# Order of k's transposes and scale sums in a shared PSUM bank, and a longer conversion pipeline for the second half of w_out

## The chip, the cores and the metric

The kernel runs on one core of one Trainium2 chip (trn2). The metric is the device time of one execution in microseconds; for the kernel before, the median of three runs is 1304.76 us (1302.74 to 1306.25). A profile is taken of one execution of its own, and every time in the trace counts from the start of that execution's span.

The engines are named as the profile names them: PE is the matrix engine (PEld its weight loads), ACT the scalar engine, DVE the vector engine, POOL the general one, SP the queue that issues the DMAs. Each engine works through its own instructions in the order in which the program lists them, and semaphores hold an instruction back until what it needs is done.

## The reference

Attention with a sigmoid in place of the softmax, and behind it a two-layer network whose activation is h - tanh(h):

```python
scores = scale * np.matmul(q, k.transpose(0, 1, 3, 2)) - np.log(S)   # q, k, v: (8, 12, 448, 64)
attn = 1.0 / (1.0 + np.exp(-scores))
attn_out = np.matmul(attn, v)
x = attn_out.transpose(0, 2, 1, 3).reshape(B * S, H * D)              # (3584, 768)
h = x @ w_in                                                          # w_in: (768, 2048)
g = h - np.tanh(h)
out = g @ w_out                                                       # w_out: (2048, 768)
```

All of it is float32 in and out. The weights w_in and w_out arrive as 8-byte words (the host views float64 data as uint64), and the kernel turns them into float32 with integer operations.

## The kernel before, in words

**Numbers in two halves.** Most products run in float16 with each operand split into a high and a low half, `F*S` rounded and the rest, where S is a power of two. So each operand needs a scale, and each scale comes from a bound on its size: a sum of squares or of magnitudes. For q, k and v of a pair of heads the sums of squares are made by ACT (`norms`, lines 299 to 306), and one small matmul with a matrix of ones adds them over the partitions and hands the total to all 128 partitions (`scales`, line 313, two or three columns). A chain of tiny instructions makes the scales from it: ACT's Relu (line 315, tile `tn`), then on DVE lines 97, 318, 320, 322 and 326. `parts` (lines 329 to 338) uses them to write the two halves of K or Q out of the transposed tile.

**Batches.** There are 8 batches. The attention of batch 0 runs first, in float32, while w_in is converted (`attention32`). From then on the work is pipelined over batches: while the two layers of batch b run on PE (`moe1` or `moe1_32` for h and g, `moe2` for the output), the attention of batch b+1 is done in pieces by a generator, `stream` (lines 424 to 529). It treats 42 pairs of heads (g = 0 to 41, six for each of the batches 1 to 7). For batch 1 the weights a stay float32 (`av32`, line 393); from batch 2 on they are split too (`split_a`, `av`, lines 371 to 389).

**One pair of heads** is two blocks of `stream` (lines 502 to 527). The block with i = 1 first turns k of the pair two ahead (`turn_k`, line 448), the block with i = 0 turns q of the next pair (line 507). Then come two score tiles (`scores`, line 359), their sigmoids on ACT (`weigh`, line 368), the halves of K or Q (lines 334, 336, 337), the products with v of the block before (`do_av`), and for i = 1 the squares of the pair three ahead.

**The bank.** `turn_k` takes one PSUM tile, `kT`, of the pool tag `tr`, of which there is one buffer: one bank of 512 float32. Its columns 0 to 447 receive the four transposes of k (line 296), its columns 448 to 450 the sums (lines 312, 313). In the kernel before, `turn_k` calls `scales` first, so the small matmul is ahead of the transposes on PE, and `scales` also lists ACT's Relu, which reads columns 448 to 450 of the same bank. The framework that places the semaphores treats accesses to one bank by different engines as ordered, whatever the columns. The next tile with the tag `tr` (`qT`, or the next `kT`) has to wait until DVE has read the low half of K or Q out of the one before it (line 337).

**The conversion of w_out** (`convert`, lines 194 to 206) is a software pipeline over 16 pieces for each half of the columns. Its stages for one piece are a load (`conv_load`, DMA on SP), a step of waiting, `conv_sign` (ACT, line 145, writes the tile `stb`), `conv_bits` (DVE, lines 150, 151 and 154; it works on `stb` in place and writes `wo`), a step of waiting, and `conv_end` (line 177: a matmul of ones with `stb`, which adds the magnitudes over the partitions into the tile `wl`). For the first half there are two steps of waiting behind the load. In the first half the tile `stb` lies in buffers of other names; in the second it takes one of the eight buffers of the tag `x`, which also hold the attention outputs of the next batch.

**What sets the order.** The order on PE, ACT, DVE and POOL is the order of the program text; nothing reorders it. In the output layer of batch 0, which the function `first` (line 874) prepares and `second` (line 930) runs, each step is six matmuls (`moe2`, line 786), and a list of events, sorted by a number, says what is slipped in after which step: a block of `stream` after the steps 2, 5, 8, 12, 16, 20, 24, 31 and 38 (`BLOCKS0`), a step of the conversion after each of the steps 1 to 19 (`CONV` = 1.0, 19 of them), splits of w_out's first half after k + 0.5, splits of w_in from 16 on, each 0.78 later (`SPLIT`), the scale of w_out's second half at 19 (`w_out_scale(1)`, which reads `wl`), and from 19.5 on its splits. An event runs after the first step whose count is not below its number. Before that list, `first` runs four blocks of `stream` back to back, with the rest of batch 0's activation between them.

For the later batches `batch` (line 909) does the same with fewer events: blocks after the steps 8, 12, 16 and so on, and the tail of the activation after the steps 1 to 5.

The functions that the diff touches, and what calls them:

Of the kernel before, what the change touches and what calls it, by code (L numbers as in the profile page):

```python
# [34 lines left out]
class Builder:  # L35
# [2 lines left out]

    INIT = (0, 2, 3, 4, 5, 6, 7)
    SPLIT = 16, 0.78  # L40
    CONV = 1.0

    BLOCKS = (8, 12, 16, 20, 24, 28, 32, 36, 40, 44, 48, 52)
    TAIL = (1, 2, 3, 4, 5)
# [149 lines left out]
    def convert(self, part):  # L194

        ps = []
        for k, (q, staged) in enumerate(part):
            ps.append({"piece": q, "k": k, "staged": staged})
        end = [self.conv_norm, None, self.conv_end] if ps[0]["staged"] else [None, self.conv_end]
        wait = [None] * (1 if ps[0]["piece"][2] else 2)  # L200
        stages = [self.conv_load] + wait + [self.conv_sign, self.conv_bits] + end
        for t in range(len(ps) + len(stages) - 1):
            for k in range(len(stages) - 1, -1, -1):
                if stages[k] and 0 <= t - k < len(ps):
                    stages[k](ps[t - k])
            yield 1
# [217 lines left out]
    def stream(self):  # L424

        NP = self.NP
        G = (self.B - 1) * NP  # L430
        at = lambda g: (1 + g // NP, g % NP)
        splits = lambda g: at(g)[0] >= self.AV32
        qk, v, ss, sc, K, Q, vv = {}, {}, {}, {}, {}, {}, {}

        def load(g):
            if g < G:
                qk[g] = self.load_qk(*at(g))
                if splits(g):
                    v[g] = self.load_v(*at(g), self.nat, "vn", 2)

        def norms(g):
            if g < G:
                ss[g] = self.norms(qk[g] + ([v[g]] if splits(g) else []))

        def turn(g, n, name):
            return self.transpose(qk[g][n], name) if g < G else None

        def turn_k(g):
            if g >= G:
                return None  # L450
            t = self.ps.tile([P, 512], F32, name="kT", tag="tr", bufs=1)
            sc[g] = self.scales(ss.pop(g), t)
            return self.transpose(qk[g][0], "kT", t=t)

        def parts_k(g, t):
            if g < G:
                K[g] = self.parts(t, sc[g][0][:, 0:1], "K", not splits(g) and g not in (2, 3))

        def parts_q(g, t):
            if g < G:  # L460
                Q[g] = self.parts(t, sc[g][0][:, 1:2], "Q", True)
                qk.pop(g)

        def prep_v(g):
            if g >= G:
                return
            if splits(g):
                vv[g] = self.prep_v(v.pop(g), sc[g][0])
            else:
                vv[g] = self.load_v(*at(g), self.att, "vhl", 3)  # L470

        load(0)
        load(1)
        yield 0, False
        norms(0)
        norms(1)
        yield 0, False
        for g in range(2):
            parts_k(g, turn_k(g))
            yield 450, False  # L480
            parts_q(g, turn(g, 1, "qT"))
            load(g + 2)
            yield 450, False
        norms(2)
        norms(3)
        yield 0, False
        todo = []

        def do_av():
            for g, c, A in todo:  # L490
                if c == 0:
                    self.acc = self.ps.tile([P, 512], F32, name="acc", tag="av", bufs=1)
                    if g % NP == 0:
                        self.xs = []
                (self.av if splits(g) else self.av32)(c, self.acc, vv[g], A)
                if c == 3:
                    self.xs.append(self.evac_x(g % NP, self.acc, sc[g][1][:, 1:2] if splits(g) else None))
                    for d in (sc, K, Q, vv):
                        d.pop(g)
            todo.clear()  # L500

        for g in range(G):
            for i in range(2):
                if i:
                    t = turn_k(g + 2)
                elif g:
                    t = turn(g + 1, 1, "qT")
                pss = [self.scores(c, K[g], Q[g]) for c in (2 * i, 2 * i + 1)]
                aa = [self.weigh(pss[0], sc[g][1][:CK, 0:1])]
                if i:  # L510
                    parts_k(g + 2, t)
                elif g:
                    parts_q(g + 1, t)
                aa.append(self.weigh(pss[1], sc[g][1][:CK, 0:1]))
                do_av()
                if i == 0:
                    if g == 0:
                        prep_v(0)
                    prep_v(g + 1)
                if splits(g):  # L520
                    aa = [self.split_a(a) for a in aa]
                todo.extend((g, 2 * i + n, a) for n, a in enumerate(aa))
                if g and i == 0:
                    load(g + 3)
                elif g:
                    norms(g + 3)
                yield 2750, True
        do_av()
        yield 1150, True
# [344 lines left out]
    def first(self, rest):  # L874

        n = 4
        next(self.tail)
        self.w_out_scale(0)
        ahead = [self.split_w_out(0)]
        for k in range(n):  # L880
            next(self.blocks)
            for _ in range(2):
                next(self.tail, None)
            if k == 1:
                next(ahead[0])
            if k == 2:
                self.finish_g()
                next(ahead[0])
        next(ahead[0])
        next(rest)  # L890
        next(ahead[0])
        next(rest)
        assert n + len(self.BLOCKS0) + len(self.BLOCKS1) == 4 * self.NP + len(self.BLOCKS) - self.ALONE
        split = self.split_w_in()
        at, each = self.SPLIT
        events = [(at + k * each, lambda: next(split, None)) for k in range(self.NC * self.NB + 1)]
        events += [(k + 0.5, lambda: next(ahead[0], None)) for k in range(self.NF // 2 - 3)]
        steps = self.NF + 3
        events += [(k * self.CONV, lambda: next(rest, None)) for k in range(1, steps + 1)]
        at = math.ceil(steps * self.CONV)  # L900

        def scale():
            self.w_out_scale(1)
            ahead[0] = self.split_w_out(1)

        events += [(at, scale)] + [(at + 0.5 * k, lambda: next(ahead[0], None)) for k in range(1, self.NF // 2 + 1)]
        self.second(0, self.BLOCKS0, 2 * self.NP - n, events)
# [72 lines left out]
```

## Time and profile before

| what | value |
|---|---|
| median of three runs | 1304.76 us |
| the profiled execution: its own time | 1303.86 us |
| its span, first to last instruction | 1301.7 us |
| mean granted clock of PE | 0.990 |
| matmuls po, line 786, 2304 of them | 391.5 us |
| matmuls ph, line 668, 2016 of them | 382.6 us |
| matmuls sc, line 359, 1008 of them | 117.0 us |
| transposes kT, line 296, 168 of them | 26.1 us |
| sums in kT, line 313, 84 matmuls for 42 calls | 12.6 us |
| column sums wl, line 177, 32 of them | 10.5 us |

The page gives the busy time of each engine and, for groups of instructions, how long the engine sat idle before them and what ended that. The view of waits sums these idle times by waiter and by what it waited for; it can be asked for a stretch of time. The timeline lists instructions in order with the idle time before them in brackets. Matmuls overlap, so the shown duration of one is longer than the distance from its start to that of the next: six po matmuls take about 1 us of PE, not six times 326 ns.

In time the span falls into: batch 0's attention (to 67 us), the first layer of batch 0 in float32 (67 to 154), four blocks back to back (154 to 180), the output layer of batch 0 with the conversion (180 to 284), and then for each of the batches 1 to 7 a first layer of about 56 us and an output layer that holds the blocks of the batch after it.

### The profile page before, as it was taken

To read this page: it belongs to the slowest core of one execution; us is meant where nothing else is said; L and a number is where in the kernel's file an instruction comes from. 1 tells how busy PE (TensorE), PEld (TensorE's weight loads), DVE (VectorE), ACT (ScalarE), POOL (GpSimd) and SP (SyncE) were. 2 spreads that over 40 slices of the span, in tenths; PEclk is the share of its full clock that TensorE was granted. 3 is DMA by queue.
4 is the path that set the end of the run, shared out by engine and by line. 5 is a ranking of instruction groups with operands and counts; after the bars stand their busy time and mean duration, and the time that the engine had idled before them with its cause. 6 is when DMAs were issued, how large, how long until landed. Compare 5 with 4: busy or idle time off the path is not lost.

```text
span 1301.7 us, 20443 instructions
## 1 busy us (share of the span) xinstructions
PE 1246.9 (96%) x8011; PEld 684.5 (53%) x8011; DVE 953.9 (73%) x1488; ACT 934.4 (72%) x1311; POOL 38.3 (3%) x38
## 2 busy tenths in 40 slices
PE   9898889899899999999999999999999999999998
PEld 3244434455555555555555655555555555555555
DVE  4989888869865798566975769666985769735940
ACT  5957666858888687876877868876887768762830
POOL 0100000000000000000000000000000000000000
PEclk9999989999999999999999999999999999999999
DMA  9952145110022200221012200221002110000001
GB/s 252 291 139 77 43 131 154 41 33 2 22 63 63 54 1 16 62 56 40 1 48 62 57 7 1 62 63 47 1 22 69 50 33 1 27 13 19 1 13 31
DMA packets 114367, 70.52 MB, mean 54 GB/s; under 512 B 91872, under 2 KB 104416, under 8 KB 114272
## 3 DMA queue, kind: packets, MB, share of 16 engines
q1 hardware_dynamic: 114272, 69.23, 20.0%
q8 instruction: 63, 1.03, 0.3%
q14 instruction: 32, 0.26, 0.1%
HBM read 58.20 MB, written 11.01 MB: 53 GB/s over the span
## 4 chain that ended last, share of the span: by engine, by line
PE 77%; ACT 9%; DVE 8%; issue 3%; DMA 2%; SPq 1%; DVEq 0%; ACTq 0%
PE ph L668 29%; PE po L786 21%; PE sc L359 7%; PE acc L383 6%; PE por L824 5%; PE ph L698 3%; ACT a L368 2%; PE kT L296 2%; DMA raw<-moe_w_in 1%; PE acc L393 1%; ACT ahl L374 1%; PE qT L296 1%; DVE m L738 1%; DVE m L749 1%; DVE m L752 1%
## 5 line engine op out<-in xcount | busy, mean ns | idle before, releaser
L786 PE MATMUL po<-wo,g 128*128 128x384 f16 x2304 | 391.5, 326 | 1.0 <-ACT o L815 1.0
L668 PE MATMUL ph<-xhl,wi 128*128 128x448 f16 x2016 | 382.6, 352 | 0.0
L786 PEld LDWEIGHTS <-g 128*128 128x128 f16 x2304 | 219.4, 98 | 172.8 <-issue 32.3
L668 PEld LDWEIGHTS <-wi 128*128 128x128 f16 x2016 | 196.7, 98 | 185.0 <-issue 1.8
L368 ACT ACTIVATE a<-sc,nls,rn 112x896 f32<-112x896 f32 x168 | 180.2, 1095 | 91.6 <-PE sc L359 78.4
L375 DVE SCALAR_TENSOR_TENSOR ahl<-a,ahl 112x896 f16<-112x896 f32 x144 | 155.7, 1122 | 67.2 <-ACT ahl L374 67.2
L734 ACT ACTIVATE u<-ph,ih 128x896 f32<-128x896 f32 x64 | 64.5, 1008 | 106.1 <-PE ph L668 94.7
L374 ACT ACTIVATE ahl<-a 112x896 f16<-112x896 f32 x144 | 128.0, 939 | 0.0
L359 PE MATMUL sc<-Q,K 64*112 64x448 f16 x1008 | 117.0, 366 | 2.3 <-ACT a L368 2.3
L738 DVE SCALAR_TENSOR_TENSOR m<-ph,ihk,u 128x896 f32<-128x896 f32 x64 | 73.5, 1148 | 59.1 <-ACT th L736 58.8
L383 PE MATMUL acc<-ahl,vhl 112*64 112x448 f16 x864 | 95.5, 357 | 0.0
L652 ACT ACTIVATE g<-m,Sg 128x896 f16<-128x896 f32 x64 | 66.6, 1041 | 32.3 <-DVE m L752 27.1
L752 DVE COPY_PREDICATED m<-u,th 128x896 f32<-128x896 uint32 x64 | 77.2, 1206 | 6.9 <-ACT u L734 0.5
L653 DVE SCALAR_TENSOR_TENSOR g<-m,Sg,g 128x896 f16<-128x896 f32 x64 | 73.4, 1147 | 9.6 <-ACT g L652 9.5
L337 DVE SCALAR_TENSOR_TENSOR Q<-qT,sn,Q 128x448 f16<-128x448 f32 x42 | 28.7, 682 | 70.3 <-ACT Q L334 70.3
L359 PEld LDWEIGHTS <-K 64*112 64x112 f16 x1008 | 60.2, 129 | 36.7 <-issue 6.0
L698 PE MATMUL ph<-x,wi 128*128 128x448 f32 x192 | 76.8, 550 | 0.0
L749 DVE SCALAR_TENSOR_TENSOR m<-q,m 128x896 f32<-128x896 f32 x64 | 69.9, 1093 | 8.1 <-ACT q L748 0.7
L739 DVE SCALAR_TENSOR_TENSOR th<-ph,ih,th 128x896 f32<-128x896 f32 x64 | 73.2, 1144 | 0.0
L745 DVE SCALAR_TENSOR_TENSOR m<-q,m 128x896 f32<-128x896 f32 x64 | 69.5, 1087 | 0.0
L751 ACT ACTIVATE u<-u,b 128x896 f32<-128x896 f32 x64 | 66.7, 1043 | 3.5 <-DVE m L738 1.5
L383 PEld LDWEIGHTS <-vhl 112*64 112x64 f16 x864 | 42.8, 109 | 46.2 <-issue 24.3
(134 smaller groups left out, 1324.9 us busy)
## 6 DMA issues: line engine op xcount, KB each, us to landing
raw<-moe_w_in SPq DMA_DIRECT2D x24, 512.0 KB, 6.3
rawo<-moe_w_out SPq DMA_DIRECT2D x32, 384.0 KB, 3.8
kn<-k SPq DMA_DIRECT2D x96, 112.0 KB, 2.8
qn<-q SPq DMA_DIRECT2D x96, 112.0 KB, 2.8
vn<-v SPq DMA_DIRECT2D x48, 224.0 KB, 2.6
out<-o SPq DMA_DIRECT2D x7, 336.0 KB, 3.2
out<-o SPq DMA_DIRECT2D x7, 288.0 KB, 3.0
out<-o SPq DMA_DIRECT2D x7, 240.0 KB, 2.6
```

The costliest lines, as they stand in the source:

```text
L359: nc.tensor.matmul(ps[:CK, h, :S], K[r, w, cs], Q[r, x, :], start=(n == 0), stop=(n == len(prods) - 1))
L368: nc.scalar.activation(a, ps[:CK, :, :S], AF.Sigmoid, bias=self.nls[:CK], scale=scale)
L374: nc.scalar.activation(A[:, 0], a, AF.Copy, scale=A_SCALE)
L375: nc.vector.scalar_tensor_tensor(A[:, 1], a, A_SCALE, A[:, 0], op0=ALU.mult, op1=ALU.subtract)
L383: nc.tensor.matmul(acc[h * D : (h + 1) * D, : self.S], v[:, w, h, c, :], A[:, x, h], start=(c == 0 and n == 0), stop=(c == 3 and n == 2),)
L653: nc.vector.scalar_tensor_tensor(g[:, 1], m, Sg, g[:, 0], op0=ALU.mult, op1=ALU.subtract)
L668: nc.tensor.matmul(ph[:, e, :S], self.wi[:, c * self.NB + k, part, e * P : (e + 1) * P], xhl[c][:, x, :], start=(i == 0), stop=(i == 3 * s ...
L698: nc.tensor.matmul(ph[:, e, :S], self.where("in", c)[:, f * P : (f + 1) * P], xs[c], start=(c == 0), stop=(c == self.NC - 1),)
L738: V.scalar_tensor_tensor(m, ps, ihk, u, op0=ALU.mult, op1=ALU.mult)
L749: V.scalar_tensor_tensor(m, q2, C2, m, op0=ALU.add, op1=ALU.mult)
L752: V.copy_predicated(m, u.bitcast(U32), th)
L786: nc.tensor.matmul(po[i][:, :H], gs[f // 2][:, x, f % 2, tk * P : (tk + 1) * P], self.wo[:, i * self.NF + f, w], start=(f == 0 and n == 0) ...
```

## The change

In `turn_k` the four transposes are listed first, and `scales`, with the small matmul and all that hangs on it, behind them. Both still go to the same tile. In `convert` the pipeline for the second half of w_out gets one more step of waiting between `conv_bits` and `conv_end`; for the first half and for w_in the list of stages comes out as it was. The conversion then has 20 steps behind the first two instead of 19, and `CONV` = 0.95 puts the twentieth at 19.0, where the nineteenth was; the steps 1 to 19 still fall after the same matmul steps.

```diff
-    CONV = 1.0
+    CONV = 0.95
...
-        end = [self.conv_norm, None, self.conv_end] if ps[0]["staged"] else [None, self.conv_end]
-        wait = [None] * (1 if ps[0]["piece"][2] else 2)
+        end = [self.conv_norm if ps[0]["staged"] else None, None, self.conv_end]
+        wait = [None, None]
+        if not ps[0]["staged"]:
+            (wait if ps[0]["piece"][2] else end).remove(None)
         stages = [self.conv_load] + wait + [self.conv_sign, self.conv_bits] + end
...
             t = self.ps.tile([P, 512], F32, name="kT", tag="tr", bufs=1)
+            turned = self.transpose(qk[g][0], "kT", t=t)
             sc[g] = self.scales(ss.pop(g), t)
-            return self.transpose(qk[g][0], "kT", t=t)
+            return turned
...
-        steps = self.NF + 3
+        steps = self.NF + 4
```

`NF` is 16. The code looks at the first piece of a conversion: its `piece[2]` is 0 for w_in and for the first half of w_out, and 1 for the second half of w_out; `staged` is true for w_in alone.

## The prediction

> **What bounds the kernel now.** I read the page first, then the waits of PE, over the whole span and by stretches, then the timeline around single turns of k.
>
> ```profile
> span 1301.7 us, 20443 instructions
> PE 1246.9 (96%) x8011; PEld 684.5 (53%) x8011; DVE 953.9 (73%) x1488; ACT 934.4 (72%) x1311; POOL 38.3 (3%) x38
> ```
>
> PE is busy for 1246.9 of 1301.7 us, so 54.8 us is all that waiting can give back, apart from matmuls that run slowly. The waits of PE over the whole span:
>
> ```profile
> PE kT L296 <- ACT tn L315: 32.5, 42, 3.6
> PE wl L177 <- DVE stb L151: 4.5, 3, 2.7
> ```
>
> All 42 turns of k wait: the transposes stand behind ACT's Relu, which reads three columns of their bank. That is 32.5 us, over half of PE's idle time. The same view for 340 to 1302 us (the later batches), then for 100 to 272 us (batch 0 with the conversion):
>
> ```profile
> PE kT L296 <- ACT tn L315: 17.9, 34, 2.2
> ...
> PE kT L296 <- ACT tn L315: 14.6, 8, 3.6
> PE wl L177 <- DVE stb L151: 3.6, 2, 2.7
> ```
>
> So there are two cases: 34 turns with short waits (17.9 us) and 8 turns with long ones (14.6 us). They have to be costed apart, because the other engines are loaded differently. The busy times by stretch (length, then PE, PEld, DVE, ACT, POOL, and the granted clock):
>
> ```profile
> 100.00:154.50 54.50, 51.14 (x152) 26.56 (x150) 50.37 (x71) 37.40 (x54) 0.00 (x0) 0.97 0.24 67
> 154.50:180.50 26.00, 17.70 (x89) 7.95 (x88) 17.81 (x37) 19.22 (x26) 0.00 (x0) 0.74 0.22 62
> 180.50:201.00 20.50, 17.45 (x104) 8.99 (x103) 18.33 (x40) 13.16 (x25) 1.22 (x1) 0.92 0.59 183
> 100.00:272.00 172.00, 150.73 (x748) 78.55 (x747) 143.58 (x276) 124.82 (x213) 4.93 (x4) 0.93 0.30 87
> 340.00:1146.00 806.00, 788.10 (x5489) 448.07 (x5487) 598.13 (x889) 626.48 (x866) 25.01 (x22) 1.00 0.15 37
> ```
>
> In the later batches DVE is busy for 598.13 of 806 us and ACT for 626.48: PE alone is the bound, and what PE does not wait is gained. From 100 to 272 us DVE has 143.58 of 172, in single stretches 92% and 89%: there a wait removed from PE can come back as a wait for DVE.
>
> **The change part by part: the 34 later turns.** One of the ordinary turns, PE and the engines that answer, then PE's weight loads, and at last a column sum and the product behind it:
>
> ```profile
> 532.37 0.28 PE L313 MATMUL kT<-ss,onesf 112*128 112x3 f32 x2
> 532.69 0.26 ACT L315 ACTIVATE tn<-kT,tiny 128x3 f32<-128x3 f32 x1 [0.45 <-PE kT L313]
> 533.01 0.60 PE L296 MATMUL kT<-ident,kn 112*128 112x112 f32 x4 [0.35 <-ACT tn L315]
> 533.54 1.34 PE L359 MATMUL sc<-Q,K 64*112 64x448 f16 x12
> 534.36 2.09 ACT L368 ACTIVATE a<-sc,nls,rn 112x896 f32<-112x896 f32 x2 [1.40 <-PE sc L359]
> ...
> 532.21 0.35 PEld L313 LDWEIGHTS kT<-ss,onesf 112*128 112x128 f32 x2
> ...
> 198.73 0.33 PE L177 MATMUL wl<-stb,onesb 128*128 128x384 bf16 x1
> 198.91 1.14 PE L786 MATMUL po<-wo,g 128*128 128x384 f16 x6
> ```
>
> Before, 1.17 us pass from the sums (532.37) to the scores (533.54): 0.64 for sums and wait, 0.53 for the transposes. After, the transposes start at once, take the same 0.53, and the pair of small matmuls follows. What that pair costs between transposes and scores no row shows. From below: 0.17, the length of a column-sum step (198.73 to 198.91), since two matmuls with two loads will not beat one with one. From above: 0.45, both loads (0.35) and 0.1 until the scores' first weights are in. I take 0.35, the two loads, which is nearest because the matmuls of three columns hardly stream. So an ordinary turn goes from 1.17 to 0.88 and saves 0.29 of its 0.35 of waiting; each turn pays 0.06 for the pair having lost the cover of the wait. Over 34 turns that is 17.9 - 34 x 0.06 = 15.9 us, with the ends 17.9 + 34 x 0.12 = 22.0 and 17.9 - 34 x 0.16 = 12.5.
>
> [...]
>
> Next in line behind the moved pair: ACT's Relu waits for it, and behind Relu in ACT's queue stand the sigmoids. The sums now end 0.53 later, so Relu starts at about 532.37 + 0.53 + 0.32 + 0.03 = 533.25 and ends at 533.5. The sigmoid waits for its scores anyway; they move 0.29 earlier, from 534.36 to 534.07. So Relu is hidden with some 0.55 us to spare. DVE's scale chain and K come later by the same 0.55, but K of this pair is needed two pairs on, and the tag's buffer only by the next block's turn of q. Nothing else moves on any queue: `scales` issues no DMA.
>
> Where the wait was long, ACT was late, and something else may be late next. The worst of the later turns:
>
> ```profile
> 344.28 0.24 ACT L315 ACTIVATE tn<-kT,tiny 128x3 f32<-128x3 f32 x1
> 344.57 0.60 PE L296 MATMUL kT<-ident,kn 112*128 112x112 f32 x4 [2.16 <-ACT tn L315]
> 345.93 2.09 ACT L368 ACTIVATE a<-sc,nls,rn 112x896 f32<-112x896 f32 x2 [1.41 <-PE sc L359]
> 349.18 2.08 DVE L375 SCALAR_TENSOR_TENSOR ahl<-a,ahl 112x896 f16<-112x896 f32 x2
> 352.32 1.33 PE L383 MATMUL acc<-ahl,vhl 112*64 112x448 f16 x12
> ```
>
> PE gains about 2.1 us here, so the products at 352.32 would come at 350.2. Their second half needs what DVE finishes at 351.26, and DVE runs without a pause before that; it would be wanted at 350.85. So 0.4 to 0.5 us is given back. ACT gains 1.41 at the same time, because the scores are ready when it comes out of Relu; so its backlog shrinks and the next turns are clean. Later batches: 15.9 - 0.5 = 15.4 us.
>
> **The 8 early turns and the column sums.** Four blocks back to back (154 to 180), then the conversion:
>
> ```profile
> 161.58 1.01 PE L296 MATMUL kT<-ident,kn 112*128 112x112 f32 x4 [2.89 <-ACT tn L315]
> 162.52 2.49 PE L359 MATMUL sc<-Q,K 64*112 64x448 f16 x12
> 163.93 2.22 ACT L368 ACTIVATE a<-sc,nls,rn 112x896 f32<-112x896 f32 x2 [2.40 <-PE sc L359]
> 176.70 2.22 ACT L368 ACTIVATE a<-sc,nls,rn 112x896 f32<-112x896 f32 x2 [2.40 <-PE sc L359]
> 191.84 0.33 PE L177 MATMUL wl<-stb,onesb 128*128 128x384 bf16 x1 [2.69 <-DVE stb L151]
> 198.04 0.68 DVE L337 SCALAR_TENSOR_TENSOR K<-kT,sn,K 128x448 f16<-128x448 f32 x1 [0.71 <-ACT K L334]
> 201.20 0.55 PE L296 MATMUL qT<-ident,qn 112*128 112x112 f32 x4
> ```
>
> From 154.5 to 180.5 PE and ACT wait for each other in turn: PE 2.89 for Relu, then ACT 2.40 for scores that run at half pace (2.49 against 1.34 above, clock 0.74). With the transposes first, the scores are done before ACT gets to Relu, so ACT loses neither 2.40: gain 4.8. ACT's idle time, 26.00 - 19.22 = 6.8, is the upper end, one of the two, 2.4, the lower.
>
> From 100 to 154.5 two of the turns lie in a stretch in which DVE has 50.37 of 54.50. PE moves ahead, but the score buffers that it needs are freed by DVE. Of DVE's 4.1 us I count 2.5 as usable; ends 1 and 4.1.
>
> From 180.5 to 201 the column sum that waited 2.69 goes one step later, behind a block, so its bits are there. But then PE runs into the turn of q at 201.20, which needs the bank that DVE empties at 198.72, and DVE pauses only 0.71 ahead of that. So the gain is 201.20 - 198.72 = 2.5, and a new wait, qT for DVE's K, of about 2.5 us appears; ends 0.4 and 3.7. The extra step holds `stb` longer: at step 16 four of them and four attention outputs fill the eight `x` buffers just to the brim. A ninth would make ACT wait for PE, which the trace shows once for a column sum, in the first half. I cost it at nothing, for no sign of the conversion falls behind step 16.
>
> The last stretch holds the one long wait:
>
> ```profile
> 225.64 0.33 PE L177 MATMUL wl<-stb,onesb 128*128 128x384 bf16 x1 [0.92 <-DVE stb L151]
> 228.43 0.61 ACT L212 ACTIVATE wo<-wo,swo_s 128x384 f16<-128x384 f32 x1 [3.60 <-DVE swo_s L231]
> 230.66 0.60 PE L296 MATMUL kT<-ident,kn 112*128 112x112 f32 x4 [3.59 <-ACT tn L315]
> 231.19 2.46 PE L359 MATMUL sc<-Q,K 64*112 64x448 f16 x12
> 251.88 0.60 PE L296 MATMUL kT<-ident,kn 112*128 112x112 f32 x4 [1.69 <-ACT tn L315]
> ```
>
> 0.92 goes: with `CONV` 0.95 the last piece's bits stand ahead of the second split of w_in on DVE, where they stood behind it; in steps 16 to 19 the conversion passes splits on ACT and DVE, and no DMA is passed. The last two column sums fall in one step, 0.18 apart, so the scale is no later. 3.59 goes, since Relu stands behind splits that wait for the scale, and PE need not wait for it; with it 2.46 - 1.34 = 1.1 of slow scores; then 1.69 and two waits of an ordinary turn's 0.35. Together 8.0, of which I count 7, because DVE must still finish the splits; ends 3 and 8.
>
> Sum for 100 to 272: 2.5 + 4.8 + 2.5 + 7 = 16.8, less 8 x 0.06 = 0.5 for the pair and 0.3 for a clock that stays low behind the new wait: 16.0, with ends of about 6 and 22. PE's waits there and DVE's 172.00 - 143.58 = 28.4 of idle time both lie above it.
>
> **The sum.** 15.4 + 16.0 = 31.4 us. The profiled execution took 1303.86 (2.16 more than its span), which gives 1272.5; it lay 0.9 below the median of 1304.76, so I forecast 1273.4.
>
> **The rivals.** *DVE keeps the start.* PE's gains from 100 to 272 come back as waits for K's bank, for w_out's splits or for the halves of x, and only 6 of the 16 stay: 1283.4. For it speaks the 92%; against it that the splits have slack and ACT is freed as well. *The pair is dear.* If it costs PE the full 0.64 behind the transposes, the ordinary turns gain nothing: 17.9 - 34 x 0.35 - 0.5 = 5.5, and the start 16 - 8 x 0.29 = 13.7, so 1285.5. The two loads of 0.35 speak against it. *The order is kept.* If the bank still ties the transposes to ACT some other way, nothing happens: 1304.8. Behind the reordered pair no PE write to that bank remains, which speaks against it. *Relu holds up ACT (slower).* Relu stands 0.88 later in PE's order, in front of the sigmoids. If scores are ready before Relu ends, each turn puts off the sigmoids, the products with v and the next buffer of scores; 42 x 0.88 = 37 against the 32.5 saved gives 1304.8 + 4.5 = 1309.3. It decides only where the 0.55 us of spare time is gone; the 1.40 that ACT waits for scores behind Relu speaks against it.
>
> **How the numbers follow.** The forecast's sum holds with 0.70 (its own range 1262 to 1280), DVE at the start 0.16, the dear pair 0.07, the order kept 0.04, slower 0.03. A measurement of this kernel can tell about 0.3%, or 3.9 us, from no change. Faster by more than that: 0.93; within it: 0.04; slower: 0.03. The range runs from 1262 (both upper ends together: 21.5 + 22 us, 1261.3) to 1288, which takes in the second and the third case.
>
> **What would show it.** Right: no wait of kT for tn; line 313 between line 296 and line 359; turns of 0.8 to 0.95 us in place of 1.17; ACT's wait for line 313 up, its wait for scores shorter; a new wait of qT for DVE's K near 195 us; the first layer of batch 1 about 16 us earlier. Wrong: kT waiting for DVE, products with v waiting for ahl in every block, or ACT's sigmoids starting later than 1.99 us behind the turn's start.

## The result and the profile after

The changed kernel takes 1266.3 us in the median (1264.9 to 1267.78, four runs) against 1305.08 (1302.74 to 1306.25) for the kernel before on the same chip: ratio 0.9705, 95% interval 0.9688 to 0.9723. In two later comparisons the ratio was 0.9694 (0.9674 to 0.9715) and 0.9698 (0.9684 to 0.9712). The forecast was 1273.4 us in a range of 1262 to 1288: the right way and inside the range, but 38.8 us were gained where 31.4 were forecast.

The page of the changed kernel. Lines below `turn_k`'s and `convert`'s edits have moved down by two or three: the transposes are now line 298, the sums 315, Relu 317, the scores 361, the sigmoid 370, the products with v 385 and 395, po 789, ph 671.

```profile
span 1262.7 us, 20448 instructions
PE 1234.1 (98%) x8011; PEld 683.9 (54%) x8011; DVE 953.0 (75%) x1488; ACT 933.0 (74%) x1311; POOL 37.9 (3%) x38
```

The span is 39.0 us shorter. PE's idle time fell from 54.8 to 28.6 us, and PE's busy time fell too, by 12.8. Of these, 8.1 lie between 100 us and the first layer of batch 1, where the granted clock rose from 0.94 to 0.98, and 5.0 between that layer and the last first layer, where the clock is 1.00 in both: there the small pair now runs in part under its neighbours (in the turn shown below it starts at 507.41, before the transposes end at 507.58). The waits of PE over the whole span (waiter, what it waited for, us, times, longest):

```profile
PE wl L177 <- DVE stb L151: 3.3, 6, 0.9
PE qT L298 <- DVE K L339: 2.7, 2, 2.2
PE sc L361 <- ACT a L370: 2.5, 1, 2.5
...
PE kT L298 <- DVE Q L339: 1.7, 2, 0.9
...
PE por L827 <- ACT o L818: 1.1, 2, 0.6
PE po L789 <- ACT o L818: 1.0, 2, 0.5
```

The line of kT waiting for tn, 32.5 us before, is gone, and for 340 us to the end the view names only the last two lines, which belong to the end of the last batch. One ordinary turn of k, followed by a turn of q, on PE:

```profile
507.03 0.55 PE L298 MATMUL kT<-ident,kn 112*128 112x112 f32 x4
507.41 0.30 PE L315 MATMUL kT<-ss,onesf 112*128 112x3 f32 x2
507.64 1.34 PE L361 MATMUL sc<-Q,K 64*112 64x448 f16 x12
508.91 1.33 PE L385 MATMUL acc<-ahl,vhl 112*64 112x448 f16 x12
...
514.08 0.55 PE L298 MATMUL qT<-ident,qn 112*128 112x112 f32 x4
514.56 1.34 PE L361 MATMUL sc<-Q,K 64*112 64x448 f16 x12
515.83 1.32 PE L385 MATMUL acc<-ahl,vhl 112*64 112x448 f16 x12
```

From the first transpose to the scores the turn of k takes 0.61 us, where 1.17 passed before. Up to the products with v it takes 1.88, the turn of q 1.75: the sums cost PE 0.13.

Where the gain lies in time is read from the starts of the first layers in the chain that ended last (start, length, what); of before the first, second, third and last, then of after the same:

```profile
283.81 54.60 PE ph L668 x288
448.42 54.60 PE ph L668 x288
598.62 47.79 PE ph L668 x252
1185.76 54.59 PE ph L668 x288
```

```profile
266.40 54.60 PE ph L671 x288
423.91 54.59 PE ph L671 x288
570.94 54.59 PE ph L671 x288
1146.92 54.59 PE ph L671 x288
```

Up to the first of them 17.4 us were gained. From the first to the last it is 901.95 - 880.52 = 21.4: 7.1 in the batch with the long waits (164.61 to 157.51), 3.2 in the next (150.20 to 147.03), and much the same after it.

### The profile page after: what moved, and what is told of

Its sections match the earlier page's. It is cut to its first block, busy times and chain, and to the rows that moved or that the text cites. A ratio compares the mean times of both kernels' runs of the same rounds, so it can differ in the third digit from the quotient of the medians.

```text
span 1262.7 us, 20448 instructions
## 1 busy us (share of the span) xinstructions
PE 1234.1 (98%) x8011; PEld 683.9 (54%) x8011; DVE 953.0 (75%) x1488; ACT 933.0 (74%) x1311; POOL 37.9 (3%) x38
## 4 chain that ended last, share of the span: by engine, by line
PE 76%; DVE 16%; ACT 4%; issue 3%; DMA 1%; SPq 0%; DVEq 0%; ACTq 0%
PE ph L671 30%; PE po L789 26%; PE sc L361 6%; PE acc L385 5%; PE por L827 3%; DVE ahl L377 2%; DVE xhl L621 2%; PE acc L395 2%; ACT a L370 1%; PE qT L298 1%; DVE sta L151 1%; DVE xhl L620 1%; DVE stb L151 1%; PE kT L298 1%; DVE wi L154 1%
## 5 line engine op out<-in xcount | busy, mean ns | idle before, releaser
L370 ACT ACTIVATE a<-sc,nls,rn 112x896 f32<-112x896 f32 x168 | 179.7, 1094 | 45.8 <-PE sc L361 38.6
L339 DVE SCALAR_TENSOR_TENSOR Q<-qT,sn,Q 128x448 f16<-128x448 f32 x42 | 28.6, 682 | 66.8 <-ACT Q L336 66.7
```

The lines of the kernel that those rows point to most:

```text
L370: nc.scalar.activation(a, ps[:CK, :, :S], AF.Sigmoid, bias=self.nls[:CK], scale=scale)
```

## The experiments

The theory after the result: PE waited because ACT's Relu read the bank into which the transposes were to write; with the transposes first nothing on PE stands behind Relu; the gain is the wait plus what the small pair hides under its neighbours; and in the start VectorE sets how much of it stays. Its rivals are named with each run.

**The two parts apart.** The first kernel has only the edit in `turn_k`, the second only those in `convert`, `CONV` and `steps`.

> Only the order in turn_k is changed; the conversion keeps its old steps. Theory (VectorE sets the pace between 175 and 195 us, so the column sums' extra step only moves PE's wait from one place to another): the column sum waits again, about 2 us or more for the bits, but the following transposes of q then wait less for K, and the time stays within 2 us of the full change, ratio to the kernel before 0.969 to 0.973. Rival (the two parts add up): the 3.6 us of waits for the bits come back in full, ratio 0.973 to 0.975.

> Only the conversion is changed; the sums stay ahead of the transposes. Theory: PE loses the 2.7 us wait for the bits but runs into ACT's Relu or K's bank soon after, so at most 2 us are gained, ratio 0.998 to 1.001; the waits of kT for tn stay at about 30 to 35 us. Rival (the waits for the bits are gained in full, with the slow matmuls behind them): 3.6 to 5.5 us, ratio 0.9958 to 0.9972.

The turn alone: 1267.04 us against 1303.01, ratio 0.9719 (0.9706 to 0.9732). The conversion alone: 1302.52, ratio 0.9998 (0.9989 to 1.0006), no change. PE's waits from 100 to 272 us with the conversion alone:

```profile
PE kT L298 <- ACT tn L317: 18.8, 8, 3.1
PE sc L361 <- ACT a L370: 2.3, 1, 2.3
PE kT L315 <- DVE Q L339: 1.0, 1, 1.0
```

The 3.6 us of waits for the bits are gone, and the eight waits of kT have grown from 14.6 to 18.8: the gain went straight into the next wait, so the rival that the waits come back in full falls. Whether the conversion adds something once the transposes are out of the way, one comparison could not tell; the next was made on one chip in the same rounds.

> The changed kernel on the same chip and in the same rounds as the next two, so that the conversion's share can be read: ratio to the kernel before 0.968 to 0.972.

> The order in turn_k alone once more, beside the full change. If the conversion's step is worth something once the transposes no longer wait, this lies 1.5 to 4 us above the full change; if VectorE sets the pace there whatever the column sums do, the two lie within 1 us.

The change: 1264.79 us, ratio 0.9698 (0.9684 to 0.9712). The turn alone: 1267.88, ratio 0.9715 (0.9699 to 0.973). The difference, 3.1 us, has the sign of the first comparison (0.9719 beside 0.9705), but the intervals overlap: 2 to 3 us are likely and not settled. The traces of these two kernels suggest a mechanism. The change first, then the turn alone:

```profile
185.85 0.33 PE L177 MATMUL wl<-stb,onesb 128*128 128x384 bf16 x1 [0.89 <-DVE stb L151]
189.83 0.60 PE L298 MATMUL qT<-ident,qn 112*128 112x112 f32 x4 [2.19 <-DVE K L339]
190.36 1.34 PE L361 MATMUL sc<-Q,K 64*112 64x448 f16 x12
191.63 1.72 PE L395 MATMUL acc<-a,vn 112*64 112x448 f32 x8
```

```profile
184.06 0.48 PE L177 MATMUL wl<-stb,onesb 128*128 128x384 bf16 x1 [3.67 <-DVE stb L151]
184.34 0.95 PE L296 MATMUL kT<-ident,kn 112*128 112x112 f32 x4
185.47 2.49 PE L359 MATMUL sc<-Q,K 64*112 64x448 f16 x12
187.88 2.80 PE L393 MATMUL acc<-a,vn 112*64 112x448 f32 x8
```

From 175 to 195 us DVE is busy for 17.96 us in both, so DVE's pace is the same. But the wait for the bits is one piece of 3.67 us, and behind it twelve scores take 2.49 us in place of 1.34 and eight products 2.80 in place of 1.72. With the extra step the waits are 0.89 and 2.19, and the matmuls behind them run at full pace in this execution. The granted clock in that stretch was 0.83 for the turn alone and 1.00 for the change. Not all of the difference between these two traces is the conversion's: the first layer of batch 1 starts at 266.04 us in the change and at 269.38 in the turn alone, but 1.2 of these 3.3 us are there at the first turn of k (103.38 and 104.60), before any of w_out's second half is converted.

**More steps of waiting.** The third kernel of those rounds has one more step of waiting:

```diff
+        end[2:2] = [] if ps[0]["staged"] or not ps[0]["piece"][2] else [None]
...
-    CONV = 0.95
+    CONV = 0.9
...
-        steps = self.NF + 4
+        steps = self.NF + 5
```

> The change, with two further steps of waiting between the bits and the column sums in place of one, and CONV 0.9, so that the last column sums stay where they are and from the tenth step on the loads and bits come one step earlier. Theory (VectorE sets the pace, the column sums only show it): the column sums' waits of 2 to 3 us fall below 1.5 us, the time stays within 1.5 us of the full change. Rival (each step of waiting is worth 2 us more): 2 us or more below the full change. If buffers of the tag x run out, ACT waits for the column sums and it is slower.

1268.1 us, ratio 0.9723 (0.9707 to 0.9739): 3.3 us above the change beside it, outside what the theory allowed, and hardly for want of buffers, since ACT waits for a column sum only once in that stretch, for 0.3 us. The waits for the bits fell to 0.9 us in total, and most of the waiting came out in one piece a little later:

```profile
190.48 1.01 PE L299 MATMUL qT<-ident,qn 112*128 112x112 f32 x4 [3.54 <-DVE K L340]
191.42 2.49 PE L362 MATMUL sc<-Q,K 64*112 64x448 f16 x12
193.84 3.00 PE L396 MATMUL acc<-a,vn 112*64 112x448 f32 x8
```

The transposes of q start at 190.48 here and at 189.83 in the change: DVE frees the bank when it does. What differs is that behind a single wait of 3.54 us the matmuls ran at about half pace (the scores 2.49 in place of 1.34, granted clock 0.87 from 175 to 195 us), and behind two shorter ones, in that execution, they did not (1.34, clock 1.00). So the theory of VectorE's pace holds for the wait, and lacked a price for what follows it. That this price makes the 2 to 3 us is argued, not shown: in the profile of the change that the page above is from, the eight products behind the wait of 2.2 us took 3.12 us too. Its next turn of k came at 199.90 us against 198.66 in another execution of the same kernel, though it had been 0.4 ahead, and its first layer of batch 1 at 266.40 against 266.83. Later waits had taken in that delay of 1.6 us whole.

**Bank or order.** The sums stay first, but go to a bank that is free at that point:

```diff
-            turned = self.transpose(qk[g][0], "kT", t=t)
-            sc[g] = self.scales(ss.pop(g), t)
-            return turned
+            own = self.ps.tile([P, 512], F32, name="own", tag="av", bufs=1)
+            sc[g] = self.scales(ss.pop(g), own)
+            return self.transpose(qk[g][0], "kT", t=t)
```

> The sums stay ahead of the transposes as in the kernel before, but go to the bank of the tag av, which is free at that point; the conversion is as in the change. Theory (the wait was for the shared bank, not for the order as such): kT no longer waits for tn, the turn takes 0.6 to 0.8 us, and the time is that of the change or up to 3 us either way, ratio 0.968 to 0.973; in its place the products with v may wait for Relu in the few turns in which ACT is late. Rival (the order itself matters, because the transposes' weight loads stand behind the small matmuls): most of the gain is missing, ratio above 0.985.

1271.61 us, ratio 0.9757 (0.9741 to 0.9772). Its ordinary turn on PE, and its waits from 100 to 272 us:

```profile
497.76 0.28 PE L315 MATMUL own<-ss,onesf 112*128 112x3 f32 x2
497.90 0.58 PE L298 MATMUL kT<-ident,kn 112*128 112x112 f32 x4
498.41 1.34 PE L361 MATMUL sc<-Q,K 64*112 64x448 f16 x12
```

```profile
PE acc L395 <- ACT tn L317: 4.3, 3, 3.1
PE own L315 <- DVE x L403: 2.8, 2, 1.4
```

With the order of the kernel before and another bank the transposes follow the sums at once, and the turn takes 0.65 us: it was the bank. The time fell short of what I expected by 3 us or more, and the second fence says where: the products with v share the new bank and now wait for Relu in three turns in which ACT is late, and the sums wait for the bank themselves. The first layer of batch 1 starts at 270.88 us instead of 266.40; from there to the last one it is 881.48 against 880.52. The change puts Relu behind all of PE's writes to the bank, so that nothing on PE stands behind it.

**The price of the pair.** In `scales` the matmul stands in a loop of two:

```diff
-        nc.tensor.matmul(pb, self.onesf[:CK, :], ss, start=True, stop=True)
+        for _ in range(2):
+            nc.tensor.matmul(pb, self.onesf[:CK, :], ss, start=True, stop=True)
```

> The change, with the pair of small matmuls for the sums issued twice in each of the 42 turns (same result). Theory (a pair behind transposes costs PE 0.22 us, read from the trace of the change): 42 x 0.22 = 9 us slower than the change, ratio to the kernel before 0.976 to 0.979. The forecast's price of 0.35: 15 us slower, ratio 0.981 to 0.983. If both loads were hidden behind other matmuls: under 3 us, ratio below 0.973.

1270.73 us, ratio 0.9747 (0.9733 to 0.976), about 5.5 us above the change; I had expected 9. An ordinary turn:

```profile
509.39 0.55 PE L298 MATMUL kT<-ident,kn 112*128 112x112 f32 x4
509.77 0.52 PE L316 MATMUL kT<-ss,onesf 112*128 112x3 f32 x4
510.22 1.34 PE L362 MATMUL sc<-Q,K 64*112 64x448 f16 x12
```

It takes 0.83 us, so the second pair costs the 0.22 that I had read. But a later batch lasts 147.92 us against 147.02, which is four times 0.22 for six turns: the rest falls into waiting that is there anyway (below). The forecast's 0.35, or 15 us, is refuted.

**Early and late turns.** In `turn_k` the pairs below 8 keep the sums first.

> The change, but only the turns of the pairs 8 to 41 have the transposes first; the 8 early turns keep the sums first. Theory (the later batches give 21.4 us by themselves, read from the starts of the first layers in the two traces, and the early turns the rest): 1303 - 21.4 = 1281.6, ratio 0.982 to 0.985. By the forecast's own sum the later batches give 15.4 us: ratio 0.987 to 0.990. Rival (the later turns profit only because the early ones do): ratio above 0.992.

1281.17 us against 1303.64, ratio 0.9822 (0.9797 to 0.9846). From its first layer of batch 1 (285.19) to that of batch 7 (1165.73) it is 880.54 us, as in the change. So the late share of about 21.4 us stands without the early one. The other 17 us are left for the early turns with the conversion; no run has these without the late turns.

**Further back still.** Two kernels issue the pair behind both score tiles. In the first, ACT's Relu stays ahead of the sigmoids; in the second `sums` is called one line later, behind the first `weigh`.

```diff
                 pss = [self.scores(c, K[g], Q[g]) for c in (2 * i, 2 * i + 1)]
+                if i:
+                    sums(g + 2, t)
                 aa = [self.weigh(pss[0], sc[g][1][:CK, 0:1])]
```

Run beside the change once more:

> The changed kernel once more, to stand beside the runs that alter it. Ratio to the kernel before 0.969 to 0.973.

> The change, but the pair of small matmuls goes still further back on PE, behind the two score tiles; ACT's Relu stays ahead of the sigmoids and so has to wait for the pair and holds the sigmoids up by about 0.9 us in each turn. Theory (PE is the bound and ACT has that much to spare in the later batches): no more than 3 us slower than the change, nearly all of it before 270 us, ratio to the kernel before 0.970 to 0.974. Rival of the prediction (what ACT loses ahead of the sigmoids comes out on PE): 42 x 0.9 = 38 us lost, ratio near 1.0; half of it would show as 0.985.

> The change, with the pair behind the two score tiles on PE and Relu behind the first sigmoid on ACT, so that it holds up nothing. K and with it the bank are ready later. Theory (the later batches do not depend on either): the later batches as in the change; in the start the sigmoids come earlier and K's bank later, so within 3 us either way, ratio 0.968 to 0.973. Rival (the bank is the next bound, the transposes of q wait for K in every pair): 42 x 0.5 us or more, ratio above 0.985.

The change: 1264.88 us, ratio 0.9694. Behind the scores: 1270.64, ratio 0.9738 (0.9714 to 0.9761). Relu behind the sigmoid as well: 1270.72, ratio 0.9742 (0.9721 to 0.9763). PE and ACT in a turn of the first of them, with PE's weight load:

```profile
498.57 0.55 PE L298 MATMUL kT<-ident,kn 112*128 112x112 f32 x4
499.05 1.34 PE L361 MATMUL sc<-Q,K 64*112 64x448 f16 x12
500.32 0.30 PEld L315 LDWEIGHTS kT<-ss,onesf 112*128 112x128 f32 x2 [0.34 <-issue]
500.32 0.39 PE L315 MATMUL kT<-ss,onesf 112*128 112x3 f32 x2
500.64 1.33 PE L385 MATMUL acc<-ahl,vhl 112*64 112x448 f16 x12
500.75 0.26 ACT L317 ACTIVATE tn<-kT,tiny 128x3 f32<-128x3 f32 x1 [1.46 <-PE kT L315]
500.91 2.08 ACT L370 ACTIVATE a<-sc,nls,rn 112x896 f32<-112x896 f32 x2
```

The sigmoids start 1.86 us behind the scores' start, where the kernel before had 534.36 - 533.54 = 0.82. That is a full microsecond of delay for ACT in each turn, yet from 340 us on PE has no wait beyond those of the change. So the slower rival's mechanism falls: in the later batches ACT has that much to spare, and moving Relu out of the way, as the second kernel does, changes nothing (its later batches take 885.63 us, the first one's 885.61). Both are nevertheless 5.1 us slower there than the change, which I had not expected. The price of the pair accounts for it: behind the scores it takes 0.32 us (500.32 to 500.64) in place of 0.13, and 34 x 0.19 = 6.5 us, of which 5.1 arrive. The fence shows its load starting only with its matmul, not ahead of it.

## Why the prediction was right, and where its terms were wrong

**The bound: right.** In the later batches PE alone was the bound; there PE is now idle for 2.0 us of 880.5 between the two first layers, where it was idle for 18.4 of 902.0, and sigmoids that started 1.86 us behind the scores' start instead of 0.82 brought PE no further wait there.

**The 34 later turns: the mechanism right, the size wrong.** The step that failed is "I take 0.35, the two loads". The pair costs 0.13 behind the transposes, less than the lower end of 0.17. That matmuls of three columns hardly stream, the reason given for 0.35, was an assumption that no run shows by itself. The lower end was taken from one matmul among full ones, and the sum set the pair behind the whole of the transposes: in the trace it starts at 507.41, before the last transpose ends (507.03 + 0.55). The transposes themselves, no longer behind a wait, take 0.48 to the next matmul in place of 0.53. So an ordinary turn went from 1.17 to 0.61, not 0.88; 17.9 + 34 x (0.56 - 0.35) would be 25.0 us. Of these 21.4 arrived, for two reasons. In the first of the 34 turns I looked for 0.4 to 0.5 us lost at the products with v; it is 0.98 at the transposes of q:

```profile
331.15 0.68 DVE L339 SCALAR_TENSOR_TENSOR K<-kT,sn,K 128x448 f16<-128x448 f32 x1
331.94 0.57 PE L298 MATMUL qT<-ident,qn 112*128 112x112 f32 x4 [0.98 <-ACT sqn L307]
```

The view names ACT's squares, but those are no input of the tile; what ends just ahead, at 331.83, is DVE's K, which frees the bank. I had seen this wait for the start only; for the later turns the prediction let K come late because the bank is wanted only by the next turn of q. And near the end of each batch two groups now stretch. From the scores at 549.93 to the products it takes 1.45 us where 1.28 passed before, and from the products of the last block at 565.41 to the next matmul 1.44 where 1.16 passed, as their second half arrives late. Together that is 0.45 in each of five batches, and with the turn of q it makes up nearly all that is missing. With the second pair of small matmuls the same two groups take 1.27 and 1.18 in the batch from 573.97: there two second pairs in each batch cost nothing. The net of 21.4 is close to the upper end that I gave, 22.0 - 0.5.

How far the pair's first load starts ahead of its matmul differs from place to place in the traces: 0.16 us in the kernel before (532.21 and 532.37), 0.09 behind the transposes (507.32 and 507.41), and not at all behind the scores, which run on 64 partitions (500.32 for both). What decides this no run shows.

**The start: the sum right, its parts not.** 17.4 us against 16.0, but by stretches, from the marks in the two traces (first scores, first po, the turn of q at 201.20, the turn at 226.78, the first layer): 4.8, of which 1.3 arose before 100 us, ahead of anything that either edit touches, then 7.7, -1.4, -0.2 and 6.6, where I had 2.5, 4.8, 2.5 and 7 for the last two together. That the parts add up to nearly the forecast is luck. PE came further ahead in the four blocks, above the end that I had set by ACT's idle time, for ACT's work there is not all tied to that stretch (ACT is busy for 19.2 us between these marks before, for 16.4 after), and gave it back at K's bank and at the bits. That is the rival "DVE keeps the start", true in part: the new wait of qT for DVE's K came where it was forecast, at 190.21 us, with 2.2 us.

**The column sums.** I put 0.92 and 2.5 us on the conversion. Alone it is worth nothing; with the turns likely 2 to 3 us. That these come from keeping the waits short, a term that was not in the sum, is argued and not shown. The eight `x` buffers held: ACT has no wait for a column sum from 150 to 268 us.

**ACT's wait for the sums** grew from 12.9 to 20.4 us, as forecast, while its wait for the scores fell from 78.4 to 38.6 us, so that it cost nothing.

## What to carry to other kernels

Here a tiny operation that shared a PSUM bank with large ones tied PE to ACT by that bank, for 32.5 us over 42 turns. With every write to the bank first and the reader on the other engine last, the wait is gone without a second bank (the turn alone, ratio 0.9719). When an engine is made faster, look for its next wait by name: alone, the conversion's step only lengthened another one, from 14.6 to 18.8 us. The price of the small pair changed with its neighbours, from 0.32 us behind the scores to 0.13 behind the transposes, and two second pairs in each batch cost nothing. So such a price is to be read from a trace with it in its new place, or bounded down to nothing.

## What the runs showed of the hardware

The same pair of three-column matmuls cost PE 0.13 us behind four transposes, 0.22 as a second pair, and 0.32 behind matmuls on 64 partitions. Behind waits of 3.54 and 3.67 us the matmuls ran at about half pace: twelve scores took 2.49 us in place of 1.34, eight products 3.00 and 2.80 in place of 1.72, and the granted clock from 175 to 195 us was 0.87 and 0.83. Behind a wait of 2.19 us the same scores and products took 1.34 and 1.72 in one execution (clock 1.00 in that stretch), and 1.59 and 3.12 in another of the same kernel (0.92). So the length of that wait alone did not decide the pace, and what did no run here shows.
